# A first-batch Sinkhorn chain of its own, Strassen blocks for the last output projection, and a new instruction order, in a fused attention and gated feed-forward kernel

## The chip, the cores and the metric

One core of one Trainium2 chip. The metric is the device time of one execution in microseconds (us), lower is better; the profile's span is some 1.8 us shorter. An execution more than 1.5% above the fastest of its kernel is called slow here, the others fast; where I compare, I compare fast ones.

## The reference, cut to what matters

```python
# q, k, v: (4 batches, 8 heads, 768 tokens, 64);  sort_net: (4, 8, 8, 8)
P = sort_net
for _ in range(5):                          # Sinkhorn: rows, then columns
    P = exp(P - max(P))
    P = P / (sum(P, axis=-1) + 1e-9)
    P = P / (sum(P, axis=-2) + 1e-9)
k_sorted = einsum('bhij,bhjcd->bhicd', P, k_blocks)     # 8 blocks of 96 tokens are mixed
v_sorted = einsum('bhij,bhjcd->bhicd', P, v_blocks)
x = softmax(q_blocks @ k_sorted.T / 8) @ v_sorted       # attention within a block
x = x.transpose(0, 2, 1, 3).reshape(3072, 512)
out = ((x @ w_a) * (x @ w_b)) @ w_out                   # 512 -> 1536 -> 512
```

So the first product with k needs the whole Sinkhorn result of its batch, and everything in the last batch ends in the output projection.

## The kernel before

The kernel describes its work as 1,176 pieces, each with an engine, a duration, the pieces it depends on and the buffers it takes. A planner gives every piece a time; a printed list, `ORDER`, says in which order the pieces are taken (it comes from an offline search). Each engine then runs its own pieces in that order, so an engine that waits for one piece cannot go on to the next. Idle TensorE time in the first 32.6 us of the plan is filled with dummy matmuls on a tile of zeros, meant to keep TensorE's clock up.

The Sinkhorn of all four batches is one chain on 32 partitions (batch and head), 64 values each:

```python
for it in range(5):
    last = add("ACT", 0.26, ... activation(out=p_nat, in_=p_nat, func=AF.Exp) ...)
    last = add("DVE", 0.21, ... reduce_sum(out=rsum, in_=p_nat) ...)
    last = add("DVE", 0.19, ... reciprocal(rsum) ...)
    last = add("DVE", 0.21, ... tensor_mul(p_nat, p_nat, rsum) ...)
    last = add("DVE", 0.26, ... reduce_sum(out=csum, in_=p_nat transposed) ...)
    last = add("DVE", 0.19, ... reciprocal(csum) ...)
    last = add("DVE", 0.21, ... tensor_mul(p_fin if it == 4 else p_nat, p_nat, csum) ...)
reps  = ...   # replicate p_fin 16 times along the columns: VectorE and ScalarE, one half each
o_pc  = ...   # eight transposing matmuls: the entries over 128 partitions
spread(nc.vector, ...)   # times a mask: s_all, the right side of the mixing matmuls
```

Gate and up products of batches 1 to 3 already use Strassen's scheme: a 2x2 block product takes 7 products in place of 8, and sums of blocks. A chain of them goes product, snapshot of the accumulator (ScalarE, 0.80 us), product into the same accumulator, and so on; two chains may be under way. The output projection was plain in every batch:

```python
STRASSEN_OUT = ()                 # out_strassen() is there, but no batch uses it
def out_plain(b, t, c, rk):       # one chunk of 128 tokens, 512 columns
    for m in range(12):
        matmul(po, lhsT=hT[..., chunk c], rhs=w_out_sb[:, m, :])
    copy PSUM -> o (VectorE or ScalarE), store
```

The softmax here doesn't subtract the row's maximum and nothing guards it: scores larger than these inputs give would overflow.

## Time and profile before

| | before |
|---|---|
| time, median of 3 (range) | 245.03 us (244.38 to 245.64) |
| span of the profiled run | 241.6 us (that run took 243.41) |
| TensorE busy | 231.0 us, of it 11 us dummies, all before 26 us |
| first product with the sorting matrix | 14.14 us |
| first gate or up product | 26.45 us |
| last matmul's end to the end of the span | 4.6 us |

TensorE bounds the kernel. The lines, and how to read them, are in the prediction below. One more table of the trace is used throughout this document. For each matmul of N columns I take N / 2.4 GHz + 2.5 ns as its work (the formula that the prediction cites and checks against the trace; less where the successor starts sooner), and what its successor starts later than that as lost. In "200 us to the last" some 0.16 us are the last matmul's own running out, in every kernel alike. Summed over the trace before, useful matmuls are 207.2 us. (A few of the 512-wide records are missing from some traces, 13 in this one and 11 in the changed kernel's; I count them by the number of instructions.) A missing record looks like 0.216 us lost, which I take out again.

### The profile page before, as it was taken

How to read it: one execution, taken by the hardware profiler on the slowest of the kernel's cores; microseconds unless marked ns; L12 is line 12 of the kernel's file. 1: busy time of each engine (PE TensorE's matmuls, PEld its weight loads, DVE VectorE, ACT ScalarE, POOL GpSimd, SP SyncE). 2: the span in 40 equal slices, each digit the busy share in tenths (PEclk: the TensorE clock that was granted, in tenths of full speed). 3: DMA queues.
4: the chain of work that ended last, by engine and by line, in shares of the span. 5: the costliest groups of instructions: out<-in, count | busy, mean ns of one | idle time of the engine just before them, and what ended most of it. 6: DMA issues, size and time to landing. Idle time of an engine off the chain costs nothing.

```text
span 241.6 us, 5320 instructions
## 1 busy us (share of the span) xinstructions
PE 231.0 (96%) x2111; PEld 130.4 (54%) x2125; DVE 154.4 (64%) x309; ACT 118.2 (49%) x177; POOL 102.0 (42%) x116
## 2 busy tenths in 40 slices
PE   8799899999999999999999999999999999999992
PEld 3367565656665445565554455556554455555440
DVE  6668649727575526699898355688872258874520
ACT  3367645675454551856674252765612066563110
POOL 8869799997500020049933020354120205433000
PEclk9999999999999999999999999999999999999998
DMA  5999999999999973509999987200009660000066
GB/s 74 173 191 135 200 167 199 199 204 198 191 203 155 126 196 100 121 1 121 151 181 175 155 197 158 45 0 4 0 0 123 140 130 0 3 0 0 0 133 130
DMA packets 54296, 28.27 MB, mean 117 GB/s; under 512 B 33536, under 2 KB 51200, under 8 KB 54272
## 3 DMA queue, kind: packets, MB, share of 16 engines
q0 software_dynamic: 26704, 14.16, 45.2%
q1 hardware_dynamic: 27568, 13.78, 29.4%
q8 instruction: 17, 0.28, 0.4%
q14 instruction: 7, 0.06, 0.1%
HBM read 30.29 MB, written 8.26 MB: 160 GB/s over the span
## 4 chain that ended last, share of the span: by engine, by line
PE 79%; DMA 8%; POOL 7%; issue 2%; DVE 1%; ACT 1%; ACTq 0%
PE ps L954 32%; PE ps L1011 26%; PE ps L860 10%; DMA v<-in_v_dram 5%; PE ps L694 3%; PE ps L572 3%; PE ps L679 3%; DMA w_a_sb<-in_moe_w_a_dram 2%; PE ps L638 1%; POOL k L440 1%; POOL s_all L523 1%; PE ps L556 1%; POOL q L428 1%; ACT f L960 1%; DVE f L374 1%
## 5 line engine op out<-in xcount | busy, mean ns | idle before, releaser
L1011 PE MATMUL ps<-w_out_sb,hT 128*128 128x512 bf16 x275 | 64.6, 379 | 1.1 <-DVE vm L319 0.2
L374 DVE TENSOR_TENSOR f<-f,ps 128x768 f32<-128x768 f32 x54 | 50.3, 951 | 15.8 <-ACT f L960 9.1
L374 POOL TENSOR_TENSOR hT<-f 128x384 bf16<-128x384 f32 x28 | 27.6, 1000 | 71.2 <-DVE f L374 71.2
L960 ACT COPY f<-ps 128x768 f32<-128x768 f32 x54 | 42.3, 801 | 29.4 <-PE ps L954 28.9
L1011 PEld LDWEIGHTS <-hT 128*128 128x128 bf16 x288 | 26.8, 98 | 29.5 <-issue 0.2
L684 ACT ACTIVATE eT<-ps 96x768 bf16<-96x768 f32 x32 | 25.2, 807 | 10.2 <-PE ps L679 9.9
L954 PE MATMUL ps<-tx,ws_a 128*128 128x384 bf16 x108 | 26.5, 327 | 0.5 <-ACT f L960 0.5
L374 DVE TENSOR_TENSOR hT<-a,ps 128x384 bf16<-128x384 bf16 x42 | 22.0, 547 | 7.7 <-ACT a L990 2.5
L954 PE MATMUL ps<-tx,ws_b 128*128 128x384 bf16 x108 | 26.4, 326 | 0.0
L317 ACT COPY o<-ps 128x512 f32<-128x512 f32 x15 | 8.8, 587 | 27.7 <-PE ps L1011 27.5
L705 DVE TENSOR_TENSOR xp<-ps,rec 96x512 bf16<-96x512 f32 x32 | 21.6, 682 | 0.7
L374 POOL TENSOR_TENSOR tx<-xT 128x768 bf16<-128x768 bf16 x3 | 4.9, 1636 | 36.7 <-DMA xT<-xp 36.7
L860 PE MATMUL ps<-xT,w_a_sb 128*128 128x384 bf16 x96 | 19.0, 327 | 0.8 <-DMA w_a_sb<-in_moe_w_a_dram 0.8
L860 PE MATMUL ps<-xT,w_b_sb 128*128 128x384 bf16 x96 | 19.1, 327 | 0.0
L954 PEld LDWEIGHTS <-ws_b 128*128 128x128 bf16 x144 | 14.1, 98 | 9.3
L954 PEld LDWEIGHTS <-ws_a 128*128 128x128 bf16 x144 | 12.7, 98 | 11.1 <-ACT f L960 2.0
L700 DVE RECIPROCAL rec<-ps 96x8 f32<-96x8 f32 x32 | 6.3, 199 | 18.3 <-PE ps L694 18.1
L317 ACT CAST kT<-ps 128x768 bf16<-128x768 f32 (+1 forms) x18 | 12.3, 696 | 11.4 <-PE ps L572 10.9
L954 PE MATMUL ps<-xT,w_a_sb 128*128 128x384 bf16 x72 | 17.6, 326 | 0.0
L954 PE MATMUL ps<-xT,w_b_sb 128*128 128x384 bf16 x72 | 17.6, 326 | 0.0
L990 ACT CAST a<-ps 128x384 bf16<-128x384 f32 x18 | 8.6, 480 | 15.7 <-PE ps L954 15.6
L374 DVE TENSOR_TENSOR hT<-f 128x384 bf16<-128x384 f32 x26 | 14.4, 555 | 2.3 <-POOL hT L374 1.2
(92 smaller groups left out, 321.7 us busy)
## 6 DMA issues: line engine op xcount, KB each, us to landing
out_dram<-o SPq DMA_DIRECT2D x48, 128.0 KB, 2.4
k<-in_k_dram POOLq DMA_DIRECT2D x16, 192.0 KB, 6.6
v<-in_v_dram POOLq DMA_DIRECT2D x16, 192.0 KB, 6.7
q<-in_q_dram POOLq DMA_DIRECT2D x20, 96.0 KB, 5.8
vd<-vm SPq DMA_DIRECT2D x10, 192.0 KB, 3.5
vs<-vd SPq DMA_DIRECT2D x10, 192.0 KB, 3.1
w_a_sb<-in_moe_w_a_dram POOLq DMA_DIRECT2D x4, 384.0 KB, 6.1
w_b_sb<-in_moe_w_b_dram POOLq DMA_DIRECT2D x4, 384.0 KB, 6.4
```

The lines of the kernel that those rows point to most:

```text
L317: nc.scalar.copy(out=out, in_=in_)
L374: ENG[eng].tensor_tensor(out=out, in0=in0, in1=in1, op=op)
L572: nc.tensor.matmul(mix[e * D:(e + 1) * D, c // 4, c % 4 * P:(c % 4 + 1) * P], lhsT=src[:, e, c * D:(c + 1) * D], rhs=s_all[:, b * H + 2 * ...
L679: nc.tensor.matmul(sc[:, e, i * BLK:(i + 1) * BLK], lhsT=kT[e * D:(e + 1) * D, at:at + P], rhs=rhs, start=True, stop=True)
L684: nc.scalar.activation(out=buf(("eT", b, p, h))[:, :, 0:HB], in_=buf(("sc", b, p, h))[0:BLK, :, 0:HB], func=AF.Exp, scale=float(scale))
L694: nc.tensor.matmul(ops_[:, e, i * OW:(i + 1) * OW], lhsT=eT[:, e, i * BLK:i * BLK + P], rhs=vs[:, h * NBH + i, e * OW:(e + 1) * OW], start ...
L705: nc.vector.tensor_tensor(out=_ap(xp, h * NBH * 2 * D, [[NB * 2 * D, BLK], [D, 2], [2 * D, NBH], [1, D]]), in0=_ap(ops_, 2, [[1024, BLK], ...
L860: nc.tensor.matmul(pf[:, u, 0:HW], lhsT=w_sb[:, kc, (m + u) * P:(m + u + 1) * P], rhs=buf(("xT", b))[:, kc, t * HW:(t + 1) * HW], start=(k ...
L954: nc.tensor.matmul(buf(key)[:, n, 0:HW], lhsT=lf(n, j), rhs=rf(j), start=start and j == 0, stop=j == 1, skip_group_check=not start)
L960: return add("ACT", 0.8, lambda: nc.scalar.copy(out=buf((name, b, g)), in_=buf(kA)[:, :, 0:HW]), [dep], get=[("f", (name, b, g))], rank=rk)
L990: e21 = add("ACT", 0.48, lambda: nc.scalar.copy(out=buf(("c21", b, g))[:, 0, :], in_=buf(kA)[:, 0, 0:HW]), [p4], get=[("a", ("c21", b, g)) ...
L1011: nc.tensor.matmul(po, lhsT=hT[:, t * 2 + m // G, m % G, c * P:(c + 1) * P], rhs=w_out_sb[:, m, :], start=(m == 0), stop=(m == KO - 1), sk ...
```

## The change

The intent: start the first mix earlier, and take 1.8 us of matmuls out of the last batch. Three parts, and another rate of dummies to go with them.

```diff
-    o_p = add("SP", ... in_=sort_net ...)                     # 32 x 64
+    o_p0 = add("SP", ... out=pa[:, 0, :], in_=sort_net[0] as "(h i) j")   # 64 x 8
+    o_p = add("SP", ... in_=sort_net[1:B] ..., [o_p0])        # 24 x 64
...
+    x = step("ACT", ... exp of pa, accum_out=ps1)             # row sums come with it
+    x = step("DVE", ... reciprocal)
+    x = step("DVE", ... p_exp = pa * pc1 * m_same)
+    x = step("PE", 0.2, sk_turn)                              # FP32 matmul: transposes each head
+    x = step("DVE", ... reduce_sum);  x = step("DVE", ... reciprocal)
+    for it in range(4):
+        x = step("ACT", ... exp(px * pc1))                    # column division folded into scale
+        x = step("PE", 0.12, sk_rows)                         # FP32 matmul: sums over a head's partitions
+        x = step("DVE", ... pr = reciprocal)
+        x = step("DVE", ... px = pa * pr, accum_out=ps1)
+        x = step("DVE", ... pc1 = reciprocal(ps1))
+    x = step("DVE", ... p_end);  o_p0 = step("PE", 0.12, spread_first)
...
     for it in range(5):                                       # batches 1 to 3, as before
-        last = add("ACT", ..., [last], rank=-9)
+        last = add("ACT", ..., [last, o_p0], rank=12)         # now after batch 0's chain
...
-            rate = 2350.0 if t > 8.5 else 1180.0              # columns of dummies per us
+            rate = 2350.0 if t > 12.4 else 1500.0 if t > 4.65 else 1180.0
...
-STRASSEN_OUT = ()
+STRASSEN_OUT = (3,)                                           # last batch's output by Strassen blocks
...
-ORDER = ( ... )                                               # another order, from a longer search
+ORDER = ( ... )
```

## The prediction

> **What bounds the kernel now.** I read the page's busy shares first, then the 40 slices, then the table of stretches, then TensorE's own timeline at both ends of the run.
>
> ```profile
> PE 231.0 (96%) x2111; PEld 130.4 (54%) x2125; DVE 154.4 (64%) x309; ACT 118.2 (49%) x177; POOL 102.0 (42%) x116
> ...
> PE   8799899999999999999999999999999999999992
> ...
> PEclk9999999999999999999999999999999999999998
> ```
>
> TensorE is busy 231.0 of 241.6 us, and its row stays at 9 from the fifth slice to the last but one. No other engine is near. So the time is TensorE's work plus what lies in front of its first useful matmul plus what lies behind its last one. But the early part is not useful work:
>
> ```profile
> 1.19 3.85 PE L1254 MATMUL ps<-ws_b 128*128 128x512 bf16 x11 [1.19 <-DVE ws_b L402]
> ...
> 11.64 1.37 PE L1254 MATMUL ps<-ws_b 128*128 128x512 bf16 x6
> ...
> 11.46 0.61 ACT L317 COPY o<-p_fin 32x512 bf16<-32x512 bf16 x1
> ...
> 12.95 0.36 PE L518 MATMUL ps<-ident,o 32*128 32x32 bf16 x8
> ...
> 14.14 0.53 PE L572 MATMUL ps<-s_all,k 128*64 128x128 bf16 x12
> ```
>
> The matmuls on ws_b are dummies that keep the clock up. Apart from transposes of q, the first real product, k with the sorting matrix, starts at 14.14 us. What it waits for is the Sinkhorn chain on VectorE and ScalarE: exp at 2.31, one iteration each 1.76 us (row sums start at 4.58, 6.34, 8.10, 9.87), replication done at 12.07 us, the spreading matmuls only at 12.95 (dummies issued ahead of them ran until 12.95), the first spread 13.42 to 13.84. After 14.14 hardly anything is lost:
>
> ```profile
> 14.00:17.00 3.00, 2.95 (x88) 2.27 (x89) 2.62 (x6) 2.67 (x6) 2.06 (x3) 1.00 1.31 193
> 17.00:20.00 3.00, 2.95 (x63) 2.09 (x61) 2.49 (x7) 2.29 (x5) 3.00 (x2) 1.00 1.23 176
> 20.00:23.00 3.00, 3.00 (x93) 2.49 (x88) 2.44 (x7) 2.74 (x7) 2.99 (x4) 1.00 0.79 89
> ...
> 29.00:32.00 3.00, 2.25 (x24) 1.36 (x23) 0.85 (x3) 0.72 (x2) 2.98 (x4) 1.00 1.18 171
> ...
> 226.00:237.00 11.00, 10.94 (x50) 4.80 (x49) 2.52 (x5) 2.10 (x4) 0.00 (x0) 1.00 0.45 96
> 237.00:241.60 4.60, 0.00 (x0) 0.00 (x0) 0.00 (x0) 0.59 (x1) 0.00 (x0) 0.79 0.54 115
> ```
>
> Columns: length, busy of TensorE, weight load, VectorE, ScalarE, GpSimd, clock, DMA share, GB/s. Three readings. TensorE has one hole, 0.75 us at 29 to 32 us, put down to a load of w_a. In 20 to 23 us the DMA falls to 89 GB/s: GpSimd, which issues the loads, is in its spreads of the later batches (three of 2.0 us). In 226 to 237 us TensorE is full of output matmuls while VectorE is idle three quarters of the time; then 4.6 us are left for one copy (0.59) and the last stores (2.4 each).
>
> **What the Trainium skill says.** "TensorE: Matmul & The Clock Gate", section "Back-to-back issue gap", gives N/2.4 + 2.5 ns per warm matmul of N columns: 216 ns at 512, 162.5 at 384, 109 at 256. The trace agrees where it can: 48 output matmuls lie between 182.59 and 192.95 us, 216 ns each; 120 of the 384-wide take 19.54 us, 163 ns. So halving the width costs nothing extra. The same page, "What's actually happening", says the clock is halved until some 3.4 us of activity; here the first eleven 512-wide dummies take 350 ns each, those at 11.64 us about 216. "FP8 and Floating Point Precision", section "TensorE Precision Notes", gives true FP32 four passes; this kernel has no FP32 matmul, so no run shows it yet, and with 8 columns it should stay near 0.25 us. "SBUF — State Buffer", section "SBUF: two separate sides", calls the port pair of VectorE and GpSimd an exclusive lock; the trace does not separate that, but the kernel serialises such work already, and GpSimd is slow at it (hT<-f 1.00 us against 0.56 on VectorE).
>
> **The change, part by part.**
>
> *Batch 0's Sinkhorn apart.* Removed from the front: five iterations of one exp and six VectorE steps on 32 partitions, two replications, eight transposing matmuls. Added: a chain on 64 partitions (head and row) of 8 columns. Its column normalisation is folded into the next exp's per-partition scale; sums across partitions are small FP32 matmuls. Durations from like rows, all estimates: exp 0.26; small reciprocal 0.17 to 0.20 (0.19 at 32x8); multiply 0.21 to 0.25 (0.21); reduction 0.17; a hop between VectorE and ScalarE or to the next VectorE step 0.03; TensorE back and forth 0.10 + 0.25 + 0.11 (0.11 is the gap from 13.31 to 13.42). Opening: exp 0.29, reciprocal 0.20, multiply 0.28, matmul 0.46, reduction 0.20, reciprocal 0.20: 1.6 us. Each of four loops: exp 0.31, matmul 0.46, reciprocal 0.23, multiply with sum 0.29, reciprocal 0.20: 1.5, in all 6.0 us. End: multiply 0.28, matmul 0.36, first spread 0.42, hop 0.10: 1.15 us. Sum 8.7 us from 2.31, so the first mix at 11.0, and I take 11.2 for dummies or queueing in between. The gain at the front is 14.14 - 11.2 = 2.9 us, of which 0.8 is the wait behind dummies; the lower rate at which dummies are now issued (1500 columns per us up to 12.4 us) should remove that.
>
> *Later batches.* Their 35 steps (30 on VectorE, some 6.3 us; 5 on ScalarE) move from an empty stretch to beside batch 0's attention, where VectorE is 80 to 90% busy. They have until batch 1's first mix, at 39.08 us before. The eight spreading matmuls, 0.36 us, move onto TensorE's full time. I charge 0.36 + 0.4 for what they delay.
>
> *Loads.* Work 2.9 us earlier wants w_a and w_b 2.9 us earlier. The dip at 20 to 23 us is about 2 us of lost transfer, and GpSimd's spreads now must come later, so the loads can move up. I keep 2.2 of the 2.9 us after the 0.76 above, and count nothing extra for the hole at 29 us.
>
> *Output of batch 3.* Removed: 6 chunks of 12 matmuls, 72 x 0.216 = 15.55 us. Added: 3 chunks x 7 products x 6 = 126 x 0.109 = 13.73 us. TensorE gain 1.8 us, all on the path that sets the end. Added elsewhere: 24 sums of hT (0.33 on VectorE as an estimate from 0.56 for 768 bf16 columns; about 0.9 on GpSimd), 8 of w_out (0.55), 12 additions out of PSUM (0.42, between the fixed and the 0.55 of 384 columns), 9 copies on ScalarE (0.37), against 6 copies of 0.59 to 0.69 removed. VectorE gets at most 7.9 + 4.4 + 5.0 = 17.3 us more, minus 2 us of removed copies. It has 11.5 us free in 180 to 200, 4.7 in 196 to 219, 12 in 219 to 237: enough, but the sums of the last block of hT (three dependent ones, about 1.3 us) and each chunk's chain (product, snapshot 0.37, product, ...) must be covered by other chunks' products. Three chunks of 4.6 us in flight with eight banks should nearly do it. I charge 0.6 us of holes.
>
> *The end.* The last stores now leave from two queues, and the last copy is 0.42 instead of 0.59: about 0.5 us off the 4.6.
>
> Sum: -2.2 - 1.8 + 0.6 - 0.5 = -3.9 us. The new order replaces a searched order and I give it 0.1. 245.0 - 4.0 = **241.0 us**.
>
> **The rivals.** (1) *Loads take the place of the Sinkhorn wait.* For it: DMA moves about 195 GB/s, its level at full use, in nearly all of 10 to 75 us, the chain of waits runs through loads until 39 us, and TensorE already waits 0.75 us for w_a. Against: the 89 GB/s stretch, and 38 us of gate and up products that need only the weights. If true the front gains 0.5 to 1 and the time is about 242.5. (2) *VectorE becomes the bound in 11 to 30 us*, because 6.3 us of Sinkhorn fall into time in which it is 80 to 90% busy, or in the last 20 us. For it: 2.62 and 2.72 of 3.0 us busy. Against: VectorE is 0.85 of 3.0 us in 29 to 32 and TensorE has other work. Then 242.5 to 243. (3) *Strassen's tail stalls*: snapshots and the reuse of a bank serialise the last chunk. Each exposed step costs 0.5 to 0.8 us; with three, the 1.8 us are gone and the time is about 243. (4) *The search pays*: all holes (0.75, 0.6 at 39 us, the dummies after 14.14, about 1.1 us) close and the front keeps the full 2.9: about 239.
>
> **Range and chances.** Rivals 1 to 3 rarely come together, and even then the front and TensorE's 1.8 us leave something; rival 4 adds about 2. 8 times in 10 within 239.2 to 243.2. 2% is 4.9 us, i.e. below 240.1, which needs all I count and one of the holes: 0.26. Slower by 2% would need a new stall of 9 us: 0.01. Within 2%: 0.73.
>
> **What will show it.** The first matmul of k with s_all at 11.0 to 11.5 instead of 14.14; if it is later, the chain was mis-sized, and its small matmuls' and accumulating steps' durations tell where. The start of batch 0's gate and up products near 24 instead of 26.45, batch 1's first mix before 37: if they stay, rival 1. In 20 to 26 us the DMA near 195 GB/s. At the end 126 matmuls of 256 columns with 109 ns between starts, TensorE's holes between 225 us and its last matmul below 0.6 us in sum (else rival 3), last matmul to end of the span about 4.1 us. The prediction is wrong if TensorE's idle time after the first mix grows by more than 1 us, or if the clock falls in the front for want of dummies.

## The result, and the profile after

| | before | after |
|---|---|---|
| time, median (range), 4 runs each | 245.33 us (244.38 to 246.27) | 242.41 us (241.86 to 242.99) |
| profiled run: time, span | 243.41, 241.6 us | 242.99, 241.1 us |
| first product with the sorting matrix | 14.14 us | 12.67 us |
| first gate or up product | 26.45 us | 27.79 us |
| useful matmul work, whole program | 207.2 us | 205.4 us |
| of it done by 40 us, by 60 us | 20.4, 37.8 us | 20.6, 38.0 us |
| lost between matmuls, 60 to 200 us | 7.1 us | 7.2 us |
| lost between matmuls, 200 us to the last | 0.4 us | 2.0 us |
| last matmul to end of span | 4.55 us | 4.50 us |

The ratio is 0.9881, 95% interval 0.9834 to 0.9928. A ratio here is the mean time of one kernel's fast runs over that of the other's fast runs of the same rounds, so not quite the ratio of the medians. The gain is some 1.2%, and real.

Mind one thing in the table: the profiled run of before, 243.41 us, was faster than every timed one (243.73 to 247.83), and that of after its slowest of four. So the two traces differ by 0.5 us where the medians differ by 2.9.

The changed kernel's page, busy shares and two rows of slices:

```profile
PE 229.5 (95%) x2167; PEld 135.2 (56%) x2180; DVE 153.3 (64%) x338; ACT 119.9 (50%) x189; POOL 142.6 (59%) x152
...
PE   8799988999999999999999999999999999999992
...
PEclk9999999999999999999999999999999999999999
```

TensorE fell by 1.5 us only. GpSimd rose by 40: the order gave it 13 more products hT<-f (13 us), and the sums that Strassen's output needs, of w_out (13 us) and of hT (11 us). Then the front, from the timeline (start, duration, engine, line, operation; in brackets what the engine waited for):

```profile
2.68 0.21 ACT L537 ACTIVATE pa<-pa 64x8 f32<-64x8 f32 x1 [0.66 <-DMA pa<-in_sort_net_dram]
2.80 0.19 ACT L537 ACTIVATION_READ_ACCUMULATOR pa<-pa 64x1 f32 x1
3.02 0.15 DVE L539 RECIPROCAL pc<-ps 64x1 f32<-64x1 f32 x1 [0.48 <-ACT pa L537]
3.12 0.07 DVE L443 MEMSET kT<- 128x16 uint32 x1
...
3.91 0.21 DVE L448 MEMSET vs<- 96x32 bf16 x4
4.04 0.24 DVE L531 SCALAR_TENSOR_TENSOR p_exp<-pa,pc,m_same 64x64 f32<-64x64 f32 x1
4.71 0.38 PE L523 MATMUL ps<-m_row,p_exp 64*64 64x8 f32 x2
...
5.57 0.26 ACT L547 ACTIVATE pa<-ps,pc 64x8 f32<-64x8 f32 x1 [2.59 <-DVE pc L545]
...
11.21 0.28 DVE L531 SCALAR_TENSOR_TENSOR p_end<-px,pc,m_head 64x64 bf16<-64x64 f32 x1
11.96 0.20 PE L558 MATMUL ps<-p_end,m_rep 64*128 64x64 bf16 x1
...
12.67 0.53 PE L646 MATMUL ps<-s_all,k 128*64 128x128 bf16 x12
```

The four loops run from 5.57 to 11.17, 1.4 us each, as cheap as hoped. The opening is what is dear. The first exp starts 0.37 us later than before, its accumulator is read by an instruction of its own, and between two steps of the chain VectorE sets pads to zero for 0.9 us: the order put that block there.

Two of the stretches that the prediction named, for the changed kernel (columns as there):

```profile
20.00:23.00 3.00, 2.84 (x68) 2.02 (x68) 2.81 (x9) 2.73 (x7) 1.15 (x3) 1.00 1.09 135
...
29.00:32.00 3.00, 2.23 (x14) 1.01 (x12) 0.39 (x2) 0.46 (x2) 2.98 (x4) 1.00 1.17 165
```

The DMA dip at 20 to 23 us is only half mended (135 GB/s where it was 89), and the hole at 29 to 32 us is still there. What GpSimd, which issues the loads, waited for from 12 to 30 us (total, times, longest):

```profile
POOL w_b_sb L486 <- DMA w_a_sb<-in_moe_w_a_dram: 3.6, 2, 3.0
POOL w_a_sb L486 <- DMA q<-in_q_dram: 3.5, 2, 2.9
```

It is free of its spreads now, but it waits for earlier loads: the program allows only so many bytes on their way. So the weights' third to eighth load land at 26.2 to 38.6 us, where before they landed at 25.7 to 37.0.

Last, the chain of waits at the end of the run, before and then after (start, length, engine, tile, line, instructions):

```profile
195.92 19.54 PE ps L954 x120
...
225.77 3.88 PE ps L1011 x18
229.71 7.30 PE ps L1011 x33
```

```profile
195.05 15.68 PE ps L1028 x96
211.67 2.14 PE ps L1028 x12
213.89 0.81 ACT f L1034
214.74 4.72 PE ps L1028 x28
...
224.20 10.64 PE ps L1178 x97
235.75 0.84 PE ps L1178 x6
```

In the chain after, a ScalarE copy of 0.81 us stands three times between TensorE's products (L1028: gate and up; L1178: Strassen's output; the third, at 221.33, is among the lines left out): a snapshot that other matmuls did not cover in full. The chain before passes one such copy, at 215.54, but all that TensorE lost there from 200 us on is the 0.4 us of the table. L1178 with 97 matmuls in 10.64 us is 110 ns a matmul of 256 columns, as predicted.

### The profile page after: what moved, and what is told of

Same layout as the page of the kernel before. It is cut to its first block, busy times and chain, and to the rows that moved or that the text cites. A ratio compares the mean times of both kernels' runs of the same rounds, so it can differ in the third digit from the quotient of the medians.

```text
span 241.1 us, 5535 instructions
## 1 busy us (share of the span) xinstructions
PE 229.5 (95%) x2167; PEld 135.2 (56%) x2180; DVE 153.3 (64%) x338; ACT 119.9 (50%) x189; POOL 142.6 (59%) x152
## 4 chain that ended last, share of the span: by engine, by line
PE 79%; DMA 8%; POOL 5%; DVE 3%; ACT 2%; issue 1%; DVEq 0%; ACTq 0%
PE ps L1028 34%; PE ps L1085 19%; PE ps L934 7%; DMA q<-in_q_dram 6%; PE ps L1178 5%; PE ps L768 3%; PE ps L753 3%; DMA vd<-vm 2%; PE ps L646 2%; PE ps L630 2%; PE ps L734 1%; POOL k L469 1%; POOL v L469 1%; ACT f L1034 1%; PE ps L712 1%
## 5 line engine op out<-in xcount | busy, mean ns | idle before, releaser
L389 POOL TENSOR_TENSOR hT<-f 128x384 bf16<-128x384 f32 x41 | 40.3, 1001 | 30.6 <-DVE f L389 29.4
L1085 PE MATMUL ps<-w_out_sb,hT 128*128 128x512 bf16 x205 | 48.5, 379 | 0.8 <-issue 0.3
L1085 PEld LDWEIGHTS <-hT 128*128 128x128 bf16 x216 | 20.0, 98 | 21.7 <-ACT eT L758 0.3
L1028 PE MATMUL ps<-tx,ws_a 128*128 128x384 bf16 x108 | 26.4, 326 | 0.3 <-ACT f L1034 0.3
L1028 PE MATMUL ps<-tx,ws_b 128*128 128x384 bf16 x108 | 26.4, 326 | 0.0
L389 POOL TENSOR_TENSOR tx<-xT 128x768 bf16<-128x768 bf16 x3 | 4.9, 1638 | 25.7 <-DMA xT<-xp 25.7
L1028 PEld LDWEIGHTS <-ws_b 128*128 128x128 bf16 x144 | 14.1, 98 | 9.3
L1028 PEld LDWEIGHTS <-ws_a 128*128 128x128 bf16 x144 | 13.1, 98 | 9.8 <-DVE f L389 1.3
L1028 PE MATMUL ps<-xT,w_a_sb 128*128 128x384 bf16 x72 | 17.6, 327 | 0.0
L1028 PE MATMUL ps<-xT,w_b_sb 128*128 128x384 bf16 x72 | 17.6, 326 | 0.0
L319 ACT CAST kT<-ps 128x768 bf16<-128x768 f32 (+1 forms) x17 | 11.7, 708 | 8.4 <-PE ps L646 7.2
L319 ACT COPY o<-ps 128x512 f32<-128x512 f32 x12 | 6.8, 587 | 17.1 <-PE ps L1085 14.3
L945 ACT CAST a<-ps 128x768 bf16<-128x768 f32 x12 | 9.4, 796 | 11.8 <-PE ps L934 11.8
L1028 PEld LDWEIGHTS <-w_b_sb 128*128 128x128 bf16 x108 | 10.6, 98 | 7.0
```

Source lines behind the costliest of these rows:

```text
L319: nc.scalar.copy(out=out, in_=in_)
L389: ENG[eng].tensor_tensor(out=out, in0=in0, in1=in1, op=op)
L945: ea = add("ACT", 0.8, lambda: nc.scalar.copy(out=buf(("a", b, t, m)), in_=buf(("pf", b, t, m, "a"))[:, :, 0:HW]), [ps_["a", 1]], get=[("a ...
L1028: nc.tensor.matmul(buf(key)[:, n, 0:HW], lhsT=lf(n, j), rhs=rf(j), start=start and j == 0, stop=j == 1, skip_group_check=not start)
L1085: nc.tensor.matmul(po, lhsT=hT[:, t * 2 + m // G, m % G, c * P:(c + 1) * P], rhs=w_out_sb[:, m, :], start=(m == 0), stop=(m == KO - 1), sk ...
```

## The experiments

Twelve runs of ten kernels, all with correct results, in three groups of four, each group on one chip with the kernel before beside it (its fast mean 244.9, 245.3 and 245.0 us).

### First group: the parts alone

My first idea was to separate the two pieces of arithmetic from the order. An order made for one set of pieces does not fit another set, so I wrote a search of my own over `ORDER` with the kernel's planner as its target, and gave every combination an order from the same search.

```diff
# s_base: the kernel before, only ORDER replaced
# s_sink: the changed kernel with   -STRASSEN_OUT = (3,)   +STRASSEN_OUT = ()   , ORDER replaced
# s_str:  the kernel before with    -STRASSEN_OUT = ()     +STRASSEN_OUT = (3,) , ORDER replaced
# s_both: the changed kernel, only ORDER replaced
```

> The kernel before with nothing but its order of issue replaced by one from a search of mine (five minutes, against the durations that the kernel's own planner uses). If the order is a share of the change's gain by itself (theory O), this is faster than before by 1 to 2 us (the planner says 1.9). If the order of before was as good as it gets on the chip (theory P: the parts, not the order), it stays within 0.5 us of 245.

> Batch 0's Sinkhorn apart, output projection plain, order from the same search with the same time. Theory P and my prediction: about 2 us faster than s_base, since the first mix comes earlier by 1.5 us or more. Theory L (loads and the copies out of PSUM bound the first 40 us, so that an earlier first mix is waited away): within 0.6 us of s_base. The planner says 1.9.

> The old Sinkhorn, output of the last batch by Strassen, same search. My prediction's terms for this part: -1.8 TensorE, +0.6 holes, -0.5 at the end: 1.7 us faster than s_base. If the chain of snapshots stalls the tail (my third rival), 0 to 0.7 us. The planner says 1.6.

> Both parts, same search. If the parts add, faster than s_base by the sum of the two gains above (3.5 to 4 us) and faster than the changed kernel, whose plan this search shortened by 3.8 us: about 239. If theory L holds, it equals s_str within 0.6 us.

| kernel | planner's end | median | ratio to before (95%) | first mix | lost, 200 us to last |
|---|---|---|---|---|---|
| s_base | 237.5 | 249.78 | 1.0177 (1.0123 to 1.0231) | 17.49 | 0.2 |
| s_sink | 235.6 | 247.66 | 1.0117 (1.0066 to 1.0168) | 13.45 | 0.4 |
| s_str | 235.9 | 244.88 | 0.9985 (0.9947 to 1.0023) | 15.46 | 0.7 |
| s_both | 233.2 | 240.06 | 0.9784 (0.9743 to 0.9825) | 13.32 | 0.4 |

(The planner's end is 239.4 for the kernel before and 237.0 for the changed one.) The base case settles something else than it was meant to. The planner called it 1.9 us better than the kernel before, and the chip made it 4.4 us worse. The trace shows where; what TensorE waited for from 8 to 80 us, then three lines of its timeline and one stretch (columns as in the prediction, the clock third from the end):

```profile
PE ps L556 <- DMA q<-in_q_dram: 4.6, 2, 4.1
PE ps L572 <- DVE vm L319: 2.5, 1, 2.5
```

```profile
11.93 0.85 PE L556 MATMUL ps<-ident,q 64*64 64x64 bf16 x24 [4.14 <-DMA q<-in_q_dram]
...
17.49 0.53 PE L572 MATMUL ps<-s_all,k 128*64 128x128 bf16 x12
...
68.99 0.53 PE L572 MATMUL ps<-s_all,k 128*64 128x128 bf16 x12 [2.46 <-DVE vm L319]
```

```profile
70.00:72.00 2.00, 2.00 (x15) 1.15 (x13) 1.97 (x5) 0.35 (x1) 0.76 (x1) 0.50 1.73 229
```

My search had put transposes of q ahead of the spreading matmuls because the planner thought their loads would be there. They were not, TensorE stood for 4.1 us, and the first mix moved to 17.49. But that is the smaller part: at 60 us s_base has done 1.6 us less useful work than the kernel before. From 60 to 80 us it loses 6.2 us between matmuls where the kernel before loses 1.7: it stands 2.5 us for a VectorE copy, and from 69.7 to 73.2 us the clock is at half (more on that below; another such stretch, from 11.7 to 15.1 us, follows the first wait). So an order alone, with not one instruction changed, can cost 4.4 us, as much as both parts of the change were to bring. The differences within this table (Strassen -4.7 without and -8.1 us with the new Sinkhorn, between fast means) therefore contain the luck of four orders and are no measure of the parts. What the group does show: useful work in the traces without missing records is 207.1 us with plain output (s_sink) and 205.3 with Strassen's, the 1.8 us predicted; and s_both, the changed kernel's very pieces in another order, is faster than the kernel before on its chip (the changed kernel did not run there; the third group compares the two).

### Second group: which wait in the changed kernel sets the end?

```diff
# after_early: pads split in two and moved behind the chain, q's transposes out of its way
#              (the moves are in ORDER, not shown)
-    o_pads = add("DVE", 1.0, pads, [o_rep], rank=1)
+    o_pads1 = add("DVE", 0.6, pads, [o_rep], rank=1)
+    o_pads = add("DVE", 0.4, pads2, [o_pads1], rank=1)

# after_late: nine idle reciprocals in the chain
-        x = step("DVE", 0.15, ... reciprocal(out=pc1, in_=ps1) ...)
+        x = step("DVE", ..., again)       # the same reciprocal four times in loops 0 to 2

# after_gate: more loads may be on their way
-            if way > (2.8e6 if len(ld_n) < 12 else 2.4e6) ...
+            if way > (2.8e6 if len(ld_n) < 12 else 3.2e6) ...
-        if len(ld_n) >= 7:
-            ds.append(ld_n[-7][0])
+        if len(ld_n) >= 9:
+            ds.append(ld_n[-9][0])

# after_plain: plain output of the last batch, in the order of the kernel before from there on
-STRASSEN_OUT = (3,)
+STRASSEN_OUT = ()
```

> The changed kernel with its first mix moved forward: the one block of clearing instructions (0.9 us on VectorE) that stood between the second and third step of batch 0's Sinkhorn is cut in two and put into later gaps, and the q transposes and copies are moved behind the chain's own steps on TensorE and ScalarE. First mix near 11.7 instead of 12.67. Theory L (the loads bound the first 40 us): the time stays within 0.4 us of the changed kernel's. Theory P (the start sets the end, as my prediction had it): 0.8 to 1 us faster.

> The changed kernel with nine idle reciprocals added to batch 0's Sinkhorn, three in each of three loops: first mix some 1.4 us later, near 14.1, where the kernel before had it. Theory L: at most 0.5 us slower than the changed kernel. Theory P: 1.2 to 1.5 us slower.

> The changed kernel with more loads under way at once: the limit of bytes raised from 2.4 to 3.2 million and of loads from 7 to 9 between the 12th and 24th load. GpSimd now stands 7.7 us in that stretch waiting for earlier loads before it issues w_a and w_b. If that limit is what makes the weights late (theory L1), w_a and w_b land 1 to 2 us earlier than 26.18 to 38.62 us, and the time falls by 0.5 to 1.5 us. If the DMA engines are simply full (theory L2), the landings and the time stay.

> The changed kernel up to the gate and up products of its last batch, instruction for instruction in the same order; then the plain output projection in the order of the kernel before. Strassen's worth alone: my terms -1.8 + 0.6 - 0.5 say it is 1.7 us slower than the changed kernel; if the tail's stalls eat Strassen (rival 3), 0 to 0.7 us slower.

| kernel | first mix | work done by 40 us | fast mean | ratio of fast runs (95%) |
|---|---|---|---|---|
| after_early | 11.24 | 20.7 | 242.40 | 0.9882 (0.9835 to 0.9929) |
| after_late | 13.95 | (slow profile) | 242.25 | 0.9879 (0.9822 to 0.9936) |
| after_gate | 12.32 | 21.3 | 242.76 | 0.9900 (0.9849 to 0.9951) |
| after_plain | 12.79 | 20.6 | 242.82 | 0.9902 (0.9855 to 0.9950) |

After_early and after_late move the first mix by 1.4 us down and 1.3 us up:

```profile
11.24 0.53 PE L650 MATMUL ps<-s_all,k 128*64 128x128 bf16 x12
```

```profile
13.95 0.53 PE L650 MATMUL ps<-s_all,k 128*64 128x128 bf16 x12
```

After_early's 11.24 lies inside the 11.0 to 11.5 that the prediction named. The fast runs do not notice: 242.4 and 242.25 us, a difference of 0.15 with a standard error of 0.7, where theory P wanted 2.0 or more. (Three of after_late's six runs were slow, so its mean is of three, and its median of all six is 245.08; more on that below.) And after_late starts its first mix only 0.2 us before the kernel before does, 14.14, and is still at 0.988 of it: in the fast runs, most of what the change gained it did not gain through an early first mix. After_gate lets the third to eighth weight load land 2 to 4 us earlier (23.8 to 34.9 us), and TensorE waits for no load between 26 and 40 us; its time is unchanged too. So neither the start of the Sinkhorn result nor the weights alone set the end, within the 1.2 to 1.5 us that five rounds resolve. What is left between them is VectorE and ScalarE, which copy every mixed block out of PSUM, the memory that matmuls write to: from 14 to 26 us they are busy for 10.1 and 10.4 of 12 us in the changed kernel, and for 10.3 and 10.1 in the kernel before. That they are the limit there is argued, not shown; I have no run that lightens them.

After_plain undoes Strassen's output. The changed kernel itself was not on this chip; by their ratios to the kernel before (0.9902 against 0.9881 and 0.9906) after_plain costs -0.1 to 0.5 us, not to be told from nothing, against 1.8 us of matmuls. So some 2.4 of the 2.9 us gained come from what lies before the tail: the Sinkhorn part and the body's order together, which no run here separates. After_plain's trace loses 0.36 us between matmuls from 200 us to the last, where the changed kernel loses 1.98. So the saving is made and 1.6 of its 1.8 us are lost again in the same stretch. Two causes remain: Strassen's chains cannot be covered, or this order does not cover them.

### Third group: the tail's order

Two orders for the same pieces are at hand, the changed kernel's and s_both's. I cut both where the last batch's gate and up products begin (about 192 us of the plan) and crossed them.

```diff
# after_again: the changed kernel         # both_again: s_both
# after_tail:  ORDER of the changed kernel up to the cut, of s_both from there
# both_tail:   ORDER of s_both up to the cut, of the changed kernel from there
```

> The changed kernel, unaltered, as the reference of this group. It was at 0.988 of the kernel before on its first chip (and its variants at 0.988 to 0.990 on a second). Both theories: 0.988, +-0.003. In its trace TensorE again loses some 1.9 us between matmuls from 210 to 238 us.

> The same pieces of work as the changed kernel in the other order that my own search found, run again because one chip gave it 0.978 and its profile fell in the slow state. If that order is really better, 0.978 +-0.003, about 2.4 us under the changed kernel on the same chip; if the first figure was luck, 0.985 to 0.988. A trace of the fast state should show under 0.6 us lost between matmuls from 210 to 238 us.

> The changed kernel's order up to about 192 us of the plan (the last batch's gate and up products begin there), from there the other order. Theory T (the tail's order gives the Strassen output's saving back, 1.9 us lost between matmuls from 210 to 238 us): the loss falls under 0.7 us, and the time falls by 1.2 to 1.6 us, to 0.982 of the kernel before. Rival B (what the better order gains, it gains in the body, before 190 us): time as the changed kernel, 0.988. The plan itself says -2.3 us.

> The mirror image: the other order up to about 192 us, the changed kernel's order from there. Theory T: it gives back 1.2 to 1.6 us of the better order's gain, so 0.984 or so, with 1.5 us or more lost between matmuls from 210 to 238 us. Rival B: 0.978, as the better order. The plan says +2.8 us against the better order whole.

| kernel | body | tail | fast mean | ratio (95%) | lost, 200 us to last |
|---|---|---|---|---|---|
| after_again | changed | changed | 242.53 | 0.9906 (0.9855 to 0.9956) | 1.98 |
| after_tail | changed | s_both | 241.45 | 0.9855 (0.9814 to 0.9896) | 0.36 |
| both_tail | s_both | changed | 241.88 | 0.9872 (0.9822 to 0.9923) | 1.91 |
| both_again | s_both | s_both | 240.57 | 0.9819 (0.9771 to 0.9867) | 0.35 |

The loss follows the tail's order and not the body's, in both crossings: 1.98 and 1.91 against 0.36 and 0.35 us. The chain of waits of both_tail, then of both_again:

```profile
208.84 0.81 ACT f L1034
209.69 2.14 PE ps L1028 x12
211.91 0.81 ACT f L1034
...
219.35 0.81 ACT f L1034
...
222.22 10.64 PE ps L1178 x97
...
```

```profile
193.70 24.74 PE ps L1028 x152
220.83 12.82 PE ps L1178 x116
```

In the better tail 152 gate and up matmuls run without a break, then the output's. In the other, the chain goes three times through a snapshot (ACT f). Those are snapshots of the gate and up chains, not of Strassen's output: at that moment both chains under way wait, and no output matmul stands in the queue before them. The fourth hole, 0.43 us before 235.75 in the changed kernel, is Strassen's own: the last product waits for a VectorE sum, with nothing left to run beside it; of this 0.10 remains in the better tail.

In time the tail's order is worth 1.08 us with one body and 1.31 with the other, 1.2 on average with a standard error of 0.5 (from the scatter of the fast runs): about what the traces say, and the 95% interval, roughly 0.2 to 2.2, excludes zero. (Fast runs too can carry stretches of half clock, see below, which blur the times; the loss between matmuls at the tail is free of them.) The body's order is worth another 0.8 with an error of 0.5, which is not settled. Both together: s_both's order beats the changed kernel by 2.0 us on this chip (error 0.7), and its two groups put it at 0.978 and 0.982 of the kernel before. It is the best version that I have, though its median on this chip, 241.35, is spoilt by two slow runs in six.

### What the slow runs are

Three profiles fell into the slow state (s_both, after_late, after_tail), and in each the trace shows TensorE at half its clock for a time. After_late, stretches of 2 us (columns as before; the granted clock is the third number from the end):

```profile
24.00:26.00 2.00, 0.66 (x19) 0.49 (x16) 0.56 (x2) 0.77 (x2) 0.80 (x3) 0.93 1.18 164
26.00:28.00 2.00, 1.55 (x21) 1.39 (x20) 0.95 (x2) 0.76 (x2) 1.64 (x1) 0.50 1.00 148
...
34.00:36.00 2.00, 2.00 (x8) 0.88 (x6) 1.51 (x8) 0.26 (x1) 1.62 (x3) 0.51 1.23 182
```

and, in its timeline, where TensorE started again after standing within that stretch:

```profile
26.45 0.32 PE L634 MATMUL ps<-ident,q 64*64 64x64 bf16 x5 [1.79 <-issue]
```

TensorE ran at half its clock from about 25.7 to 36.0 us, after a stretch in which it was busy for 0.66 of 2 us, and lost about 5 us of work by 40 us (15.6 done in place of 20.6). This is the gate that the Trainium skill describes in "TensorE: Matmul & The Clock Gate", section "What's actually happening": half rate after an idle window of some 3.4 us, full rate after a busy one. The lengths of the half-rate stretches in four traces (after_late 10.2, after_tail 6.8, both_again 3.4, s_both 3.4 us, worked out from the granted clock of each 2 us) are whole multiples of that window.

Half clock is not confined to the runs called slow. After the clock first came up, six of the eleven fast profiles have it too: s_base twice, after_early, s_sink, s_str, both_tail and both_again once, 3.4 us each. All ten such stretches in the fourteen traces begin during a stand of TensorE of at least 1.0 us or within 1.8 us of its end. All six stands of 1.8 us or more were followed by one (4.1 and 2.4 us for loads of q in s_base and s_str, 2.5 for a VectorE copy in s_base, 1.9 for a load of v in s_both, 1.8 each in s_sink and after_late), and four of the nine from 1.0 to 1.5 us. The stands in after_late and s_sink, and one of 1.1 us in after_tail, fall in the midst of a group of like matmuls, and the profile names nothing that TensorE waited for ("issue"); what they are stays open.

A mean clock below 0.985 occurred in none of the 33 runs of the kernel before in the three groups, in 2 of 10 of the changed kernel, in 3 of 6 of s_base and of both_tail. So a kernel in which TensorE comes to stand for more than about 1 us risks half clock on top of the stand. Not every slow run is of this kind: the one slow run of the kernel before (247.83 us) has a mean clock of 0.995. Whether more dummy matmuls would cure the half clock, no run here tells.

## Why the prediction was right or wrong

The time was right: 241.0 us predicted, 242.41 measured, inside the range, and "within 2%" came true. The mechanism was not, and the agreement is in good part luck: of the four terms only TensorE's 1.8 us came out. The front, the holes and the end were all too hopeful, and in the pair of traces the sum comes to -0.3 us instead of -3.9. That the medians still differ by 2.9 is due to some 2.4 us that none of the terms explains. The prediction's own sign of being wrong came true in this pair: TensorE's idle time from the first mix to its last matmul, which was not to grow by more than 1 us, grew from 3.0 to 4.4 us (3.6 in after_again).

- **Batch 0's Sinkhorn, 2.9 us at the front: half wrong.** The first mix came at 12.67, not at 11.0 to 11.5. The step that failed is the opening, worked out as 1.6 us from 2.31. It took from 2.31 to 5.57, that is 3.26: a load that landed 0.37 later, an accumulator read of 0.19 that I had not counted, 0.9 of pads in the chain, and dummies ahead of the first small matmul. The loops took 5.6 against 6.0, the end 1.5 against 1.15. As to the FP32 matmuls, with 0.28 us they are near the 0.25 that I took.
- **"I keep 2.2 of the 2.9 us": wrong in this pair of traces.** By 40 us the changed kernel had done 0.2 us more useful matmul work than the kernel before, by 60 us again 0.2. In the second profile of the changed kernel (after_again) it is 1.1 more by 60 us. The step that failed is the path: that an earlier first mix carries through to the end. After_early had its first mix at 11.24 and after_late at 13.95, and their fast runs took the same time. My signs for rival 1 came true (first gate product at 27.79, not near 24; batch 1's first mix at 51.85, not before 37; weights no earlier), but after_gate shows that earlier weights alone do not buy it back, and after_early that an earlier chain alone does not either. Rival 2, the engines that empty PSUM, is what I would now put first, unproved.
- **TensorE's 1.8 us: right.** 207.1 to 205.3 us of useful work, 110 ns a matmul.
- **"I charge 0.6 us of holes": mis-sized.** 1.6 us more are lost after 200 us than before, so rival 3 came nearly whole: by the traces Strassen's output nets 0.2 us. The sign that I had set for it, holes below 0.6 us from 225 us on, was met (0.5): the loss sat in front of that window, from 211 to 222 us. And its reason was another. I feared Strassen's own snapshots; three of the four holes are snapshots of the gate and up chains, and another order of the same pieces closes them.
- **The end, 0.5 us: wrong.** 4.55 to 4.50. The last copy did shrink, from 0.59 to 0.42, but with it and the second queue for stores what follows the last matmul hardly shortened.
- **"The new order replaces a searched order and I give it 0.1": the step that I should have looked at hardest.** With all pieces equal, orders differ by 2.0 us (s_both against the changed kernel) and by 4.4 (s_base against before). The choice of an order can weigh as much as the change's other two parts. What the change's own order is worth, no run isolates: the old order does not fit the new pieces.
- **What the sum leaves open.** Between the two traces the terms add up: work by 60 us -0.2, matmuls -1.8, the tail's holes +1.6, the middle +0.1, the end -0.05, in all -0.3 against -0.5 in the span. The medians differ by 2.9. The balance of about 2.4 lies between a fast profiled run of before and its usual runs; some of it may be front, as after_again's trace suggests. After_plain says that nearly all of the gain is made before the tail, and after_late that an early first mix is not what makes most of it; the body's order and the later batches' moved Sinkhorn are left, unseparated. I have only one trace of the kernel before, so where its usual runs lose that time stays open.

## What to carry to other kernels

When a program's engines each run a fixed order, an order is a part of the change like any other: cross the old and new orders at a stage's border before you credit arithmetic with a gain or a loss. Here a saving of matmuls in the last stage counted only where other matmuls stood ready at every snapshot, so look at the chain of waits for a copy between two products. Shortening a chain at the start is worth what the stages behind it can take up: move it both ways and see whether the end follows. And a time that comes out as predicted does not show the mechanism: check the terms.

## What the Trainium skill lacked or had wrong

- "TensorE: Matmul & The Clock Gate": it says a busy window of some 3.4 us brings the full rate back. In two traces the half rate lasted 6.8 and 10.2 us, two and three such windows, though TensorE was busy for 2.00 of every 2 us from 28 us on. How busy is busy enough, the page does not say.
- The same page: it says half rate comes after an idle window of some 3.4 us. Here it came after stands of 1.0 to 2.5 us in nine of ten cases, and four of nine stands of 1.0 to 1.5 us had it follow; how short a stand can be enough, the page does not say.
- "FP8 and Floating Point Precision": it gives true FP32 four passes. Here one FP32 matmul call (64x64 by 8 columns) shows as two weight loads and two matmul records, 0.28 us together, so the passes cannot be read off the trace's records.
- No page gives the time of an accumulated sum, though one says that it is a second instruction. In the trace that instruction takes 0.19 us after an exp on ScalarE and 0.07 us on VectorE.
